# Attention units taken two by two, routing once per batch, and the experts' second layer with activations stationary

## The chip, the cores and the metric

The kernel runs on one core of a Trainium2 chip, in float32 throughout. The metric is the device time of one execution in microseconds. Five engines share the work, each with an instruction queue of its own that it follows in order: TensorE (PE in the profile; PEld is its loading of weights), VectorE (DVE), ScalarE (ACT), GpSimd (POOL) and SyncE (SP), which here only issues DMAs.

## The reference, cut to what matters

Banded attention with a few global keys is followed by a mixture of experts, in which each token goes to the one expert with the largest logit.

```python
# q, k, v: (4, 8, 768, 64); keep = key < 8, or 0 <= query - key < 96
scores = scale * q @ k.T - slope[h] * dist            # masked where not keep
x = softmax(scores) @ v                               # -> (3072, 512), heads side by side
logits = x @ w_gate                                   # 8 experts
e = argmax(logits);  gate_w = softmax(logits)[e]
y = relu(x @ w1[e]) @ w2[e]                           # 512 -> 1024 -> 512, for each token's expert
out = gate_w * y
```

## The kernel before, in words

**Attention.** The work is cut into 48 units: 4 batches times 4 pairs of heads times 3 groups of 256 queries. A queue of loads on SyncE (`load`, line 376, eight DMAs a pair for q and k; `load_v`, two) runs three pairs ahead in two buffers. VectorE turns a pair's q and k (`turn_qk`, lines 436 and 437), ScalarE makes copies of the keys and values (`keys_at`, `turn_v`). A unit passes through `scores` (line 484: matmuls of 64 rows, for two heads at once on the two halves of the array's rows; then the exponential on ScalarE, line 487, and the product with the decay on VectorE, lines 494 and 498), two units later through `attend` (line 516, then VectorE's normalization, lines 520 and 523), and two later through `turn` (line 532: two transposes on TensorE of the unit's rows; the copy, line 535, is ScalarE's). The last pair of heads of each group stores the rows to the DRAM table `x_tok` (`store`, line 236) and computes the logits (`logits`, line 547: w_gate as 32-column weights on the four column quarters of the array, one per chunk of 128 features; `logits_sum`, line 560, adds the four quarters with a matmul). Where a batch is complete, `gate` (lines 211 to 229) takes the argmax and the gate weight.

**Routing.** `spread` (line 567 on) makes each token's place in its expert's list: prefix sums over the batch by matmuls with a triangle (line 572), with ones for each earlier chunk of the batch (line 574) and for earlier batches (line 578), then some ten small VectorE steps and two larger one-hot tables (lines 603 and 608). `spread_sum` (line 624) sums the tables into `acc`. After the last batch, `order` ranks experts 1 to 7 by their number of tokens, so that the list of capacities `CAPS` (line 22: 464, 416, 416, 400, 400, 368, 368, 272) can be static; experts are run in the order of `ORDER` (line 23). `half_0`/`fetch_0` gather the rows of expert 0, in two lots; `take(1)` those of the next expert, once `settle` and `rows_of` have made its indices.

**The order of the instructions** is written out by hand in `banded_attention` (from line 733 on, the loop at line 744). Behind the last unit, 16 pieces of expert 0's first 256 slots (`work`, `hidden_0` line 320 and `result_0` line 327) are dealt out between the steps of the routing, so that TensorE has something to do while VectorE and the DMAs work.

**Experts.** The remaining 208 slots of expert 0 and the seven other experts follow (lines 999 to 1107). `hidden` (line 1039): 32 products, w1 stationary, all slots of the expert moving, Relu by ScalarE (line 1041). `result` (line 1082): w2 stationary, hidden activations moving, so that the output comes out with features on the partitions; VectorE copies it to `yT` (line 1084), and TensorE transposes it back by blocks of 128 slots (`turn`, line 1072), which happens during the next expert's `hidden`. `finish` scales by the gate weight (line 309) and scatters the rows to the output (`put`, line 301, an indirect DMA of GpSimd).

Rows of the expert after the next are gathered by GpSimd, 32 slots times four feature chunks per DMA (`gather_one`, line 259), each made to wait for a step of the present expert (`pace`); `sort` (line 270, VectorE transposes) turns them into the operand of `hidden` and stands between `hidden` and `result`. Weights lie in two buffers, `w_first` and `w_second`; SyncE loads the next expert's by an index that it reads from `ids_s` (`fetch`, lines 240 and 1024, five DMAs of 4 MB in all), w1 as soon as `hidden` has done with the buffer and w2 as soon as `result` has. For expert 1 the load waits for the index and for half of its gathers.

Of the kernel before, what the change touches and what calls it, by code (L numbers as in the profile page):

```python
# [16 lines left out]
P = 128  # L17
# [6 lines left out]
NQ = 4  # L24
# [5 lines left out]
def kernel(  # L30
# [27 lines left out]

    x_tok = nc.dram_tensor("x_tok", (N * NJ, P), F32)
# [22 lines left out]
    q_first = consts.tile([P, NB, 2, D], F32)  # L82
# [48 lines left out]

    tokid = consts.tile([P, NC], F32)
    iota(tokid, [[P, NC]], -N, 1)
# [5 lines left out]
    def later_constants():  # L139
# [13 lines left out]
        nc.vector.tensor_copy(out=j_of, in_=j_i)  # L153
        nc.vector.memset(wg_sb, 0.0)
        nc.sync.dma_start(wg_sb[:, :, 0:E], moe_w_gate.rearrange("(kc p) e -> p kc e", p=P))

    gsum = sel[:, 0:E]

    M_ec = consts.tile([P, E, NC], F32)
    M_ce = consts.tile([P, NC, E], F32)  # L160
    rk_all = consts.tile([P, NB, E + 1], F32)
    nc.vector.memset(rk_all[:, :, E:E + 1], 0.5)
    Macc = consts.tile([P, E], F32)
# [8 lines left out]
    NR = E - 1  # L172
# [5 lines left out]
    idx_0 = [consts.tile([P, 1, 2], I32, name=f"idx_0{i}") for i in range(2)]  # L178
    gslot_0 = [consts.tile([P, 1, 2], F32, name=f"gslot_0{i}") for i in range(2)]
    rows_0 = [consts.tile([P, 2 * TB], I32, name=f"rows_0{i}") for i in range(2)]  # L180
# [75 lines left out]

    def gather_one(xq, cols, i, top=N):
# [16 lines left out]
    def plan(p):  # L274
        if p < E:
            r = ORDER[p] - 1
            xqs[p] = xq_s[p % 2]
            cols = rows_s[:, NQ * TB * r:NQ * TB * r + NQ * TB]
            for i in range(pieces_of(CAPS[r + 1])):
                pending.append((xqs[p], cols, i))  # L280
# [10 lines left out]
    taken = []  # L291

    def take(p):
        plan(p)
        while pending:
            taken.append(gather_one(*pending.pop(0)))

    scatters = []

    def put(y, rows, where):  # L300
        p = nc.gpsimd.indirect_dma_start(out=out[:, :], out_offset=bass.IndirectOffsetOnAxis(ap=where, axis=0),  # L301
                                         in_=y[0:rows, :], in_offset=None, bounds_check=N - 1, oob_is_err=False)
# [4 lines left out]
    def scaled(name, rows, po, gs, where, later=None):  # L307
        y = yp.tile([P, DM], F32, tag="y", name=name)
        nc.vector.tensor_scalar(out=y[0:rows, :], in0=po[0:rows, :], scalar1=gs[0:rows, :], scalar2=None, op0=ALU.mult)  # L309
        if later is None:  # L310
            put(y, rows, where[0:rows, :])
        else:
            later.append(lambda: put(y, rows, where[0:rows, :]))

# [9 lines left out]
    def result_0(po, q, f0, nf, later=None):  # L324
# [4 lines left out]
        if f0 + nf == FC:  # L329
            scaled(f"y_0_{q}", P, po, gslot_0[0][:, 0, q:q + 1], idx_0[0][:, 0, q:q + 1], later)  # L330
# [18 lines left out]
    def banded_attention():  # L349
        with ExitStack() as actx:  # L350
            mp = actx.enter_context(tc.tile_pool(name="maskb", bufs=1))
            xlp = actx.enter_context(tc.tile_pool(name="xlb", bufs=3))
            xrp = actx.enter_context(tc.tile_pool(name="xrb", bufs=5))
            ldp = actx.enter_context(tc.tile_pool(name="ldb", bufs=2))
# [821 lines left out]
```

## Time and profile before

| | us |
|---|---|
| three timed runs | 543.27, 543.34, 544.06 |
| span of the profiled execution | 555.3 |
| first unit of attention to the last, by the chain | 5 to 178 |
| routing of the last batch beside expert 0's first 256 slots | 178 to 214 |
| expert 0's rest, and experts 1 to 7 | 214 to 548 |
| the end | 548 to 555 |
| VectorE, ScalarE and GpSimd busy, of the span | 201.7, 132.6 and 138.3 |

The page's fifth part lists groups of instructions by line and shape with their count, busy time, and the mean time of one. Matmuls overlap in the pipeline, so the mean time of one is longer than the distance between two starts; that distance is read from the chain or the timeline, as the length of a run divided by its count. Each float32 product is two matmul instructions in these lists, and each transpose on TensorE is one. The list of waits gives, for each pair of a waiting group and the group that released it, the total, the number of times and the longest. The stretches of the experts' stage in the chain alternate: `ph` (hidden), `pt` (the transposes back) and `po` (result).

### The profile page before, as it was taken

To read this page: it belongs to the slowest core of one execution; us is meant where nothing else is said; L and a number is where in the kernel's file an instruction comes from. 1 tells how busy PE (TensorE), PEld (TensorE's weight loads), DVE (VectorE), ACT (ScalarE), POOL (GpSimd) and SP (SyncE) were. 2 spreads that over 40 slices of the span, in tenths; PEclk is the share of its full clock that TensorE was granted. 3 is DMA by queue.
4 is the path that set the end of the run, shared out by engine and by line. 5 is a ranking of instruction groups with operands and counts; after the bars stand their busy time and mean duration, and the time that the engine had idled before them with its cause. 6 is when DMAs were issued, how large, how long until landed. Compare 5 with 4: busy or idle time off the path is not lost.

```text
span 555.3 us, 8124 instructions
## 1 busy us (share of the span) xinstructions
PE 527.4 (95%) x3130; PEld 391.7 (71%) x3130; DVE 201.7 (36%) x509; ACT 132.6 (24%) x263; POOL 138.3 (25%) x161
## 2 busy tenths in 40 slices
PE   4999999999999998599999999999999999999994
PEld 3988898899898965595555555555555876666694
DVE  4758687687684443112013101211301303111012
ACT  4666456555552200101101100100110100101100
POOL 5000000000007067234224423513511716402002
PEclk9999999999999999699999999999999999999998
DMA  9999999999903014995446174372543776101001
GB/s 145 146 156 178 234 176 175 231 161 159 256 6 124 31 30 93 297 187 201 98 90 223 34 159 141 114 156 70 183 107 64 234 147 216 48 0 53 3 1 60
DMA packets 145185, 71.97 MB, mean 130 GB/s; under 512 B 126656, under 2 KB 126660, under 8 KB 145136
## 3 DMA queue, kind: packets, MB, share of 16 engines
q1 hardware_dynamic: 137344, 58.16, 50.0%
q0 software_dynamic: 5264, 12.59, 7.5%
q10 hardware_dynamic: 2528, 0.59, 0.7%
q8 instruction: 27, 0.44, 0.4%
q14 instruction: 22, 0.18, 0.1%
HBM read 59.00 MB, written 12.65 MB: 129 GB/s over the span
## 4 chain that ended last, share of the span: by engine, by line
PE 85%; DMA 5%; SPq 2%; issue 2%; DVE 2%; another core or an unknown queue 2%; POOL 1%; ACT 0%; POOLq 0%; DVEq 0%; ACTq 0%
PE po L1082 26%; PE ph L1039 26%; PE o L516 12%; PE s L484 7%; PE ph L320 3%; PE px L532 3%; PE po L327 2%; PE pt L1072 2%; SPq L384 2%; DMA xq_s<-x_tok,rows_s 2%; DMA kb<-in_k_dram 1%; PE pq L547 1%; PE pi L624 1%; PE pl L560 1%
## 5 line engine op out<-in xcount | busy, mean ns | idle before, releaser
L259 POOL DMA_INDIRECT xq_s<-x_tok,rows_s x85 | 85.4, 1005 | 151.4 <-DVE yT L1084 103.6
L1041 ACT ACTIVATE hT<-ph 128x416 f32<-128x416 f32 (+4 forms) x64 | 29.6, 467 | 294.3 <-PE ph L1039 270.1
L1039 PE MATMUL ph<-xe,w_first 128*128 128x208 f32 (+3 forms) x256 | 78.7, 465 | 8.9 <-ACT hT L1041 8.9
L1082 PE MATMUL po<-hT,w_second 128*128 128x416 f32 (+4 forms) x320 | 80.7, 412 | 2.1 <-DVE yT L1084 2.1
L1039 PE MATMUL ph<-xe,w_second 128*128 128x416 f32 (+3 forms) x256 | 80.2, 469 | 0.0
L1082 PE MATMUL po<-hT,w_first 128*128 128x208 f32 (+3 forms) x256 | 75.5, 456 | 0.0
L1082 PEld LDWEIGHTS po<-hT,w_second 128*128 128x128 f32 x320 | 56.0, 190 | 26.3 <-issue 10.2
L1039 PEld LDWEIGHTS ph<-xe,w_first 128*128 128x128 f32 x256 | 49.0, 197 | 35.2 <-issue 10.0
L516 PE MATMUL o<-vt,e 128*128 128x128 f32 x384 | 72.6, 278 | 0.0
L1039 PEld LDWEIGHTS ph<-xe,w_second 128*128 128x128 f32 x256 | 48.0, 190 | 28.1 <-issue 9.9
L1082 PEld LDWEIGHTS po<-hT,w_first 128*128 128x128 f32 x256 | 47.7, 190 | 27.1 <-issue 10.2
L270 DVE STREAM_TRANSPOSE xe<-xq_s 128x128 f32<-128x128 f32 x85 | 22.8, 293 | 117.7 <-DMA xq_s<-x_tok,rows_s 112.5
L516 PE MATMUL o<-va,e 128*128 128x128 f32 x320 | 62.8, 278 | 0.0
L1084 DVE COPY yT<-po 128x416 f32<-128x416 f32 (+6 forms) x36 | 17.0, 481 | 125.6 <-PE po L1082 125.6
L259 POOL DMA_INDIRECT xq<-x_tok,rows x15 | 17.3, 1154 | 181.0 <-DVE early L648 160.5
L516 PEld LDWEIGHTS o<-vt,e 128*128 128x128 f32 x384 | 57.5, 194 | 1.5 <-issue 1.2
L487 ACT ACTIVATE e<-s 128x1024 f32<-128x1024 f32 (+1 forms) x48 | 45.5, 947 | 46.1 <-PE s L484 46.0
L516 PEld LDWEIGHTS o<-va,e 128*128 128x128 f32 x320 | 48.7, 193 | 2.6 <-issue 2.5
L301 POOL DMA_INDIRECT out_dram<-y,idx_s x25 | 24.4, 975 | 74.4 <-DVE y L309 69.9
L498 DVE TENSOR_TENSOR e<-e,Wb 128x1024 f32<-128x1024 f32 x32 | 38.8, 1211 | 10.9 <-ACT e L487 10.8
L484 PE MATMUL s<-qT,kT 64*128 64x128 f32 x384 | 40.7, 290 | 0.9 <-ACT qT L419 0.9
L484 PE MATMUL s<-qT,kA 64*128 64x128 f32 x320 | 35.7, 301 | 2.0 <-ACT kA L403 2.0
(163 smaller groups left out, 439.1 us busy)
## 6 DMA issues: line engine op xcount, KB each, us to landing
w_second<-in_moe_w_dram SPq DMA_DIRECT2D x16, 512.0 KB
w_second<-in_moe_w_dram SPq DMA_DIRECT2D x4, 2048.0 KB
x_tok<-xr SPq DMA_DIRECT2D x24, 256.0 KB
w_first<-in_moe_w_dram SPq DMA_DIRECT2D x12, 512.0 KB
w_first<-in_moe_w_dram SPq DMA_DIRECT2D x3, 2048.0 KB
vt<-in_v_dram SPq DMA_DIRECT2D x31, 192.0 KB
qb<-in_q_dram SPq DMA_DIRECT2D x60, 96.0 KB
kb<-in_k_dram SPq DMA_DIRECT2D x60, 96.0 KB
```

The costliest lines, as they stand in the source:

```text
L259: return nc.gpsimd.indirect_dma_start(out=xq[:, i, :], out_offset=None, in_=x_tok[0:NJ * top, :], in_offset=bass.IndirectOffsetOnAxis(ap=c ...
L270: nc.vector.transpose(xe[:, :, 32 * i:32 * i + 32], xq[:, i, :].rearrange("p (k q) -> p k q", k=KC))
L301: p = nc.gpsimd.indirect_dma_start(out=out[:, :], out_offset=bass.IndirectOffsetOnAxis(ap=where, axis=0), in_=y[0:rows, :], in_offset=None ...
L320: nc.tensor.matmul(ph[:, P * f:P * f + P], lhsT=w1_0[:, 0, kc, c0:c0 + P], rhs=xe_0[:, kc, P * q:P * q + P], start=(kc == 0), stop=(kc == ...
L484: nc.tensor.matmul(ps[:, h, P * m:P * m + P], lhsT=lhsT, rhs=qT[r, P * i:P * i + P], start=True, stop=True)
L487: nc.scalar.activation(e[:, :, 0:w], ps[:, :, 0:w], AF.Exp, scale=D ** -0.5)
L498: nc.vector.tensor_tensor(out=eh, in0=eh, in1=W[:, 2 * j:2 * j + 2, P:3 * P].rearrange("p h (o c) -> p h o c", o=1).to_broadcast([P, 2, 2, ...
L516: nc.tensor.matmul(po[:, t, h, :], lhsT=pt[:, h, P * m:P * m + P], rhs=(vt if own else va)[:, c0:c0 + P], start=(m == mine[0][0]), stop=(m ...
L1039: nc.tensor.matmul(ph[:, 0:C], lhsT=w1t[:, 0, kc, P * fc:P * fc + P], rhs=xe[:, kc, 0:C], start=(kc == 0), stop=(kc == KC - 1))
L1041: done = nc.scalar.activation(hT[:, fc, 0:C], ph[:, 0:C], AF.Relu)
L1082: nc.tensor.matmul(po[:, 0:c1 - c0], lhsT=w2t[:, 0, fc, P * dc:P * dc + P], rhs=hT[:, fc, c0:c1], start=(fc == 0), stop=(fc == FC - 1))
L1084: pace(2 if dc == 0 else 1, nc.vector.tensor_copy(out=yT[:, dc, c0:c1], in_=po[:, 0:c1 - c0]))
```

## The change

It touches three places.

1. *Attention.* Units go two at a time: scores of both, then one `turn` with four transposes for the pair before, then `attend` of the two units before. The logits are computed once per batch, with w_gate as 32-column weights over four quarters of the batch's tokens, accumulated over the four feature chunks; one VectorE transpose brings tokens to the partitions (so tokens are numbered differently, which `tokid` follows). A VectorE scan makes the counts of earlier chunks and batches, so that `spread` needs two products instead of six or seven. The tables of `spread` become a step of their own (`tables`). Expert 0's weights are loaded from unit 12 on, w1 first.

2. *Expert 1 takes a fixed place*, like expert 0: its weights are loaded by `expert_w1(w1_1, ...)` near the end of attention without an index, and its rows come with the second lot of expert 0's. The buffers of these weights exist from the start; before they are filled, attention keeps q and k, the first pair's q, a mask, the transposed rows and every fourth tile of exponentials in them.

3. *Second layer.* In `result`, blocks of 128 slots of the hidden activations are stationary and all 512 columns of w2 move, so the output has slots on the partitions and needs no transposing back. A remainder of up to 96 slots is done in pieces of 32 slots: four matmuls for four quarters of the features, each with 32-column weights and 128 moving columns, whose outputs lie in the four quarters of the partitions; such a piece is scattered by rows of 128 features. `sort` of the next expert moves from before `result` into it, in parts behind the second and third blocks; there are two buffers of hidden activations instead of one, and gathers are paced two to a block.

The diff, cut to its core:

```diff
+            def logits(b):
...
                 for kc in range(KC):
+                    for g in range(TB):
+                        nc.tensor.matmul(pq[32 * g:32 * g + 32, :], lhsT=wg_sb[:, kc, :], rhs=xl[:, kc, QS * g:QS * g + QS],
+                                         start=(kc == 0), stop=(kc == KC - 1))
+                L = gp.tile([P, QS], F32, tag="L", name=f"L_{b}")
+                nc.vector.transpose(L, pq)
...
             def spread(b):
...
                 nc.tensor.matmul(pr, lhsT=tri, rhs=Mb, start=True, stop=False)
-                for c in range(NB - 1):
-                    nc.tensor.matmul(pr[:, c + 1:NB, :], lhsT=ones,
...
+                nc.tensor.matmul(pr, lhsT=ones, rhs=C_b[b][:, :, 0:NB].rearrange("p e c -> p c e"), start=False, stop=True)
...
-            for n in range(nu + 1):
...
+            for n0 in range(0, nu, 2):
+                two = (n0, n0 + 1)
...
+                if n0 > 0 and c < 2 and pr + 1 < B * NJ:
+                    turn_qk(pr + 1)
+                for n in two:
...
                     scores(n)
...
+                if n0 >= 4:
+                    turn(n0 - 4)
+                    for n in two:
+                        attend(n - 2)
+                if b > 0 and m == 2:
+                    logits(b - 1)
+                if b > 0 and m == 4:
+                    spread(b - 1)
+                if 0 < b and m == (4 if b == B - 1 else 6):
+                    tables(b - 1)
+                if 0 < b and m == (6 if b == B - 1 else 8):
+                    spread_sum(b - 1)
...
+            turn(nu - 2)
+            expert_w1(w1_1, slice(1, 2))
+            work(1)
+            logits(B - 1)
+            nc.sync.dma_start(w2_1, w2v[:, 1:2, :, :])
+            work(1)
...
             def result(p):
...
+                rest = C % P if C % P <= 3 * 32 else 0
+                nq = (C - rest + P - 1) // P
+                for q in range(nq):
+                    rows = min(P, C - P * q)
+                    po = ps_o.tile([P, DM], F32, tag="po", name=f"po_{p}_{q}")
+                    for fc in range(FC):
+                        nc.tensor.matmul(po[0:rows, :], lhsT=hT[:, fc, P * q:P * q + rows], rhs=w2t[:, 0, fc, :],
+                                         start=(fc == 0), stop=(fc == FC - 1))
+                    pace(2, finish(p, q, rows, po))
+                    if p > 0 and q > 0:
+                        sort(p + 1, q - 1, nq - 1)
+                for i in range(TB * nq, pieces_of(C) if rest else 0):
+                    pt = ps_t.tile([P, P], F32, tag="pt", name=f"pt_{p}_{i}")
+                    for fc in range(FC):
+                        for g in range(TB):
+                            nc.tensor.matmul(pt[32 * g:32 * g + 32, :], lhsT=hT[:, fc, 32 * i:32 * i + 32],
+                                             rhs=w2t[:, 0, fc, P * g:P * g + P], start=(fc == 0), stop=(fc == FC - 1))
+                    finish_piece(p, i, pt)
...
             ground()
-            sort(1)
+            sort(1, 0, 1)
             hidden(0)
+            fetch(2, 0)
             plan(2)
-            turn = result(0)
+            result(0)
+            fetch(2, 1)
...
             for p in range(1, E):
-                hidden(p, turn)
-                fetch(p + 1, 0)
-                sort(p + 1)
+                hidden(p)
+                fetch(p + 2, 0)
                 plan(p + 2)
-                turn = result(p)
-                fetch(p + 1, 1)
+                result(p)
+                fetch(p + 2, 1)
```

`hidden` also zeroes the slots that fill up its last piece, and `gates_of`, in the routing's tail, adds two small matmuls that bring the gate weights into the pieces' order.

## The prediction

> **What bounds the kernel now.** I read the page's parts 1 and 4 first, then the table of groups by shape, then TensorE's timeline of the attention stage and VectorE's around the one long wait.
>
> ```profile
> PE 527.4 (95%) x3130; PEld 391.7 (71%) x3130; DVE 201.7 (36%) x509; ACT 132.6 (24%) x263; POOL 138.3 (25%) x161
> PE 85%; DMA 5%; SPq 2%; issue 2%; DVE 2%; another core or an unknown queue 2%; POOL 1%; ACT 0%; POOLq 0%; DVEq 0%; ACTq 0%
> ```
>
> TensorE is busy for 95% of the span and is 85% of the chain that ended last. Its idle gaps over 0.15 us sum to 15.2 us: 3 at the start, 8.9 at 220, 2.06 at 457, little else. So time comes out mainly where TensorE's own instructions go away, or run side by side. Busy time overlaps in a pipeline, so I price a matmul by its pace, the distance from one start to the next. In the chain, 64 matmuls of 416 columns take 22.35 us (349 ns each); 400 columns take 336 ns, 368 take 309, 208 take 176, 512 take 429. That is 0.84 ns a column, with a floor near 112 ns: 128-column matmuls and the 8-column ones of line 560 alike. (A float32 product is two such instructions, a transpose is one.)
>
> ```profile
> 50.43 0.44 PE L532 MATMUL px<-ident,xr 128*128 128x128 f32 x2
> 50.70 0.39 PE L516 MATMUL o<-va,e 128*128 128x128 f32 x2
> ...
> 52.27 0.39 PE L516 MATMUL o<-vt,e 128*128 128x128 f32 x2
> 52.58 0.49 PE L484 MATMUL s<-qT,kA 64*128 64x128 f32 x4
> 52.91 0.39 PE L484 MATMUL s<-qT,kT 64*128 64x128 f32 x4
> 53.13 0.39 PE L484 MATMUL s<-qT,kA 64*128 64x128 f32 x4
> 53.35 0.39 PE L484 MATMUL s<-qT,kT 64*128 64x128 f32 x4
> 53.67 0.44 PE L532 MATMUL px<-ident,xr 128*128 128x128 f32 x2
> 54.04 0.64 PE L547 MATMUL pq<-xl,wg_sb 128*32 128x256 f32 x8
> 54.61 0.71 PE L516 MATMUL o<-vt,e 128*128 128x128 f32 x4
> ```
>
> Two things are to be seen. Four scores start every 0.22 us, but 0.33 passes after the first four of a unit, and 0.31 between the last pair of o and the first scores: a change of the array's shape costs about 0.1 us at each edge. And eight logit matmuls of 256 columns fit into 0.57 us, though one alone paces at 216 ns: with 32-column weights on four quarters, four run at once.
>
> ```profile
> DVE xe L270 <- DMA xq_s<-x_tok,rows_s: 112.5, 44, 10.8
> ...
> ACT hT L1041 <- remote: 10.2, 1, 10.2
> ...
> PE ph L1039 <- ACT hT L1041: 8.9, 1, 8.9
> ```
>
> The lines are from the list of waits (total, times, longest). The last two are one event at 218 us: ScalarE stands still after the first Relu of expert 0's rest, for a reason the trace does not name, and TensorE with it; TensorE's clock then is 0.50 from 222.6 for 10.2 us. It costs 8.9 + 2.2 = 11.1 us. The profiled span is 555.3, the three timed runs are 543.3 to 544.1; 555.3 - 11.1 = 544.2. I read the event as not being in the timed runs, and carry my sum to 543.3. The first line's longest is the wait at 457: VectorE sat 10.8 us on a gather that landed late, beside a load of weights, with the copies of yT queued behind.
>
> [...]
>
> **The change, attention stage (38 to 214 us).**
> (a) Two units in one go: scores, scores, four transposes, attend, attend. Per pair one set of edges goes: 0.19 at the scores, 0.05 at px, 0.09 at the end of o, together 0.34 us (a full unit now is 1.09 + 0.27 + 1.88 = 3.24, without edges 2.9). 24 pairs, the first one or two not in this order: 22 x 0.34 = -7.5.
> (b) Logits once per batch. Now each of 12 pays 0.10 (px to pq) + 0.57 + 0.44 (pl) = 1.11, 13.3 in all. Then, four times, 8 rounds of four 192-column matmuls at 0.161 plus 0.25 of edges: 6.2. -7.1. The pl sums become one VectorE transpose per batch.
> (c) Prefix sums: 54 matmuls of lines 572 to 578 at 0.11 become 16. -4.2.
> (d) gates_of: two small matmuls, four instructions with edges, +0.6.
> (e) Tail: spread of the last batch now also waits for the scan, behind a transpose and eight gate steps of about 0.24: 2.8 us after the logits, with one piece of fill (16 x 0.112 = 1.8) before it: +1.0; two gaps of 0.3 go: -0.6.
> (f) What a faster TensorE runs into. VectorE has 31.6 us busy in the batch from 81 to 123 (42.0 us), and 69 instructions with about 0.04 between them: 34 us of the 37 that are left (42.0 less 2.0, 1.8 and 1.1 of a to c). Gate, spread and tables (about 5.5 us) come in three iterations of some 6 us, two of which also turn the next pair (1.9). The transposes of the next iteration leave some 1.2 us of slack, so I take +1 a batch, three times. In the first batch the loads of pair 3 set the pace until 38 us: +1 of (a) not won. SyncE issues loads for four pairs, weights and stores in 41 us (67.1 to 108.3) almost without a break; loads end 8.6 to 11.6 us ahead of use and took 3.5 to 4.8 to land, so two or three batches can eat the lead: +1. Sum +5; 0 if the queues have room, 11 if VectorE or SyncE becomes the bound.
> Weights of expert 0 come from unit 12 on. Those of expert 1, five DMAs and 4 MB, go on SyncE's queue without an index at about 165 (the stage's end, 178, less 13), behind the last stores: nothing on the path, since the loads at 217 were needed only at 237 (as hidden(0) and result(0) would run undisturbed). SBUF shared with w1_second and w2_second: the readers are done two iterations before the next writer, 0. Expert 0's last seven gathers now run partly beside those 4 MB: seven at 1.3 us and 2 to land are 11 us, TensorE has 17 of fill, 0; landing as late as the one at 457 it would be +4 (in the 11). Expert 1's thirteen stay behind them on POOL, 0.
> Sum: -7.5 - 7.1 - 4.2 + 0.6 + 0.4 + 5 = **-12.8**.
>
> **The change, expert stage.** A block of 128 slots is 16 matmuls of 512 columns, 6.87 us (line 327 does just this: 429 ns). A piece is 16 rounds of four 128-column matmuls: 16 x 0.112 + 0.3 of edges = 2.1; between 1.8 and, with every load of weights exposed (0.22 a round), 3.8. Transposes of yT, 108 at 0.109, are gone, and a part-filled piece is paid whole:
> - expert 0's rest (208): 11.25 + 0.87 becomes 6.87 + 5.7 (three pieces): +0.4
> - 416, twice: 22.35 + 1.74 becomes 20.6 + 2.1: -1.4 each
> - 400, twice: 21.49 + 1.74 becomes 22.7: -0.5 each
> - 272: 14.7 + 1.3 becomes 15.8: -0.1, and the wait of 2.06 goes, for the sort now comes 14 us later: -2.1
> - 368: 19.8 + 1.3 becomes 20.6: -0.5; the last one, 20.9 + 1.3 becomes 20.6: -1.6
> Sum -7.7 (-5.6 and -2.1). Against it: the second half of the next expert's sort now stands behind the last block's scaling, and hidden(p + 1) needs all of it. Scaling starts 0.2 after the block and takes 0.75; transposes follow at 0.197. With seven of them: 2.5 us after the block against a piece of 2.1, +0.4, three times; with five, 0; for 272 all twelve stand there: 3.5, +1.4; behind 368 no piece covers six: +2.3. Sum +4.9. VectorE loses the 36 copies (17 us); its pieces and memsets hide under matmuls. Gathers paced two to a block, and one more scatter for a piece, leave GpSimd 17 DMAs at 1.3 us in an expert's 44 us: hidden. Stage: **-2.8** (-8 to +5).
>
> Total -15.6: 543.3 - 15.6 = **527.7**; against the profile's own span, 544.2 - 15.6 = 528.6, or 539.7 if the event at 218 comes back.
>
> **The rivals.**
> A, the sum: 527.7, own range 521 to 535; chance 0.60.
> B, the queues bind. VectorE in order, or SyncE, takes 11 instead of 5, and pieces cost 3 instead of 2.1 (8 x 0.9): 527.7 + 6 + 7.2 = 541; half of that excess gives 534. For it: VectorE at 34 of 37 us. Against: its load is uneven but its waits are short. Chance 0.20.
> C, the event at 218 is in the timed runs too, tied to the load of w_second that starts then and now comes 40 us earlier: 527.7 - 11.1 = 516.6. For it: SyncE's steps are slow in just those 10 us. Against: 555.3 - 11.1 fits the timed runs. Chance 0.12.
> D, slower: the quarters do not overlap at 128 columns, so a piece is 64 x 0.112 = 7.2 us. Eight pieces: +41, 568. It decides from 2.1 + 15.6 / 8 = 4.05 us a piece. For it: nothing here shows 128-column rounds. Against: 256-column rounds pace at 0.22 for four, and 128-column scores, two at once on halves of the rows, at 0.112 for two. Chance 0.08.
>
> A measurement of this kernel can tell about 0.2% from no change, 1.1 us. Faster 0.89 (A, C, most of B), same 0.03 (the rest of B), slower 0.08. The range goes from C into B, 516 to 538, and leaves out D and the worse part of B.
>
> **What would show it.** Right: two units of scores in a row, a pair at about 6.1 us; attention's last matmul before hidden(0) about 13 us earlier; eight pieces near 2.1 us; waits of 0.4 to 2.3 us before hidden(2), hidden(6), hidden(7) on the transposes of xe; no pt on yT. Wrong: starts of a piece's matmuls 112 ns apart one by one; TensorE waiting in attention for e, xr or kT by more than 2 us a batch; hidden(1) waiting for w_second.

## The result, and the profile after

| | before | after |
|---|---|---|
| timed runs, median (range) | 543.70 us (543.27 to 544.06) | 535.64 us (535.03 to 536.54) |
| ratio, 95% interval | | 0.9854 (0.9836 to 0.9871) |
| span of the profiled execution | 555.3 | 533.1 |

The change wins 8.1 us, where 15.6 were forecast. The experiments were run in five further sittings, each beside the kernel before; it took 545.2, 545.8, 557.0, 558.4 and 558.4 us in them, so numbers are compared within one sitting only, or as ratios.

The page of the kernel after begins:

```profile
PE 503.7 (94%) x3244; PEld 344.4 (65%) x3244; DVE 179.6 (34%) x482; ACT 127.5 (24%) x227; POOL 140.1 (26%) x163
...
PE 85%; DVE 5%; DMA 3%; SPq 3%; ACT 2%; issue 1%; POOL 0%; POOLq 0%; ACTq 0%
```

TensorE still sets the time. It is busy 20.1 us less than in the undisturbed profile of the kernel before (523.8, the first experiment below), although 114 more matmuls run; in the pieces and in the logits four run side by side (they start 7 ns apart, and a round of four comes every 109 ns with 128 columns and every 163 with 192). TensorE's timeline of a stretch of attention (start, duration, instruction, count):

```profile
92.81 1.51 PE L573 MATMUL pq<-w_second,wg_sb 128*32 128x192 f32 x32
94.25 0.49 PE L507 MATMUL s<-qT,kA 64*128 64x128 f32 x4
...
95.91 0.39 PE L507 MATMUL s<-qT,kT 64*128 64x128 f32 x4
96.23 0.66 PE L559 MATMUL px<-ident,xr 128*128 128x128 f32 x4
96.73 0.39 PE L542 MATMUL o<-va,e 128*128 128x128 f32 x2
...
99.85 0.34 PE L589 MATMUL pr<-M_b,tri 128*128 128x48 f32 x2
100.02 0.40 PE L590 MATMUL pr<-C_b,ones 128*128 128x48 f32 x2
100.35 0.49 PE L507 MATMUL s<-qT,kT 64*128 64x128 f32 x4
```

The logits of a whole batch take 1.44 us to the next scores. The transposes come four at a time, once per pair, and two products make the prefix sums. The list of waits (total, times, longest) and the chain (start, duration, group) show the expert stage:

```profile
PE ph L1065 <- DVE xe L295: 4.3, 5, 2.0
...
DVE xe L295 <- DMA xq_s<-x_tok,rows: 3.4, 4, 1.0
...
PE pt L1103 <- issue: 2.7, 1, 2.7
```

```profile
211.02 6.87 PE po L1094 x16
217.88 4.38 PE pt L1103 x153
222.26 2.65 issue
224.91 2.25 PE pt L1103 x39
227.17 0.52 PE pf L1115 x2
227.69 22.91 PE ph L1065 x64
...
436.34 0.75 DVE y L335
437.23 1.08 DVE xe L295 x6
438.39 1.05 DVE xe L295 x5
439.48 20.05 PE ph L1065 x64
...
480.22 0.62 issue
480.84 1.28 DVE xe L295 x6
482.16 20.05 PE ph L1065 x64
```

Two things cost TensorE its time here. Before five of the hidden layers it waits for the sort, 4.3 us in all: at 436 the twelve transposes stand on the path behind the scaling of the block. That was in the forecast. And in expert 0's third piece it stops after 153 of 192 matmuls, for 2.65 us, and waits for nothing that the profile shows ("issue"). That was not. VectorE's old wait of 112.5 us on gathers is down to 3.4, for the sort now comes later in VectorE's queue, behind blocks of the second layer. The page also names two DMA queues of the kind `instruction`: q8 with 27 packets and 0.44 MB, 16 KB each, and q14 with 22 packets and 0.18 MB, 8 KB each. "Fetches of instructions" below are their packets.

### The profile page after: what moved, and what is told of

Its sections match the earlier page's. It is cut to its first block, busy times and chain, and to the rows that moved or that the text cites. A ratio compares the mean times of both kernels' runs of the same rounds, so it can differ in the third digit from the quotient of the medians.

```text
span 533.1 us, 8244 instructions
## 1 busy us (share of the span) xinstructions
PE 503.7 (94%) x3244; PEld 344.4 (65%) x3244; DVE 179.6 (34%) x482; ACT 127.5 (24%) x227; POOL 140.1 (26%) x163
## 4 chain that ended last, share of the span: by engine, by line
PE 85%; DVE 5%; DMA 3%; SPq 3%; ACT 2%; issue 1%; POOL 0%; POOLq 0%; ACTq 0%
PE ph L1065 29%; PE po L1094 27%; PE o L542 12%; PE s L507 6%; PE ph L347 2%; PE px L559 2%; PE po L354 2%; DMA vt<-in_v_dram 2%; SPq L409 2%; PE pt L1103 2%; DVE xe L295 1%; PE pq L573 1%; PE pi L632 1%; DVE e L524 1%; DMA k_first<-in_k_dram 1%
## 5 line engine op out<-in xcount | busy, mean ns | idle before, releaser
L284 POOL DMA_INDIRECT xq_s<-x_tok,rows_s x72 | 72.8, 1010 | 61.8 <-ACT hT L1067 49.6
L335 DVE TENSOR_SCALAR y<-po,gslot_s 128x512 f32<-128x512 f32 (+1 forms) x17 | 12.8, 751 | 223.7 <-PE po L1094 223.7
L1094 PE MATMUL po<-w_second,hT 128*128 128x512 f32 (+1 forms) x176 | 76.2, 592 | 0.0
L1094 PE MATMUL po<-w_first,hT 128*128 128x512 f32 (+1 forms) x160 | 69.3, 592 | 0.0
L1065 PEld LDWEIGHTS ph<-xe,w_first 128*128 128x128 f32 x256 | 47.5, 190 | 29.6 <-issue 10.3
L1094 PEld LDWEIGHTS po<-w_second,hT 128*128 128x128 f32 (+1 forms) x176 | 33.2, 189 | 41.3 <-issue 40.7
L542 PE MATMUL o<-vt,e 128*128 128x128 f32 x288 | 54.6, 281 | 0.0
L1094 PEld LDWEIGHTS po<-w_first,hT 128*128 128x128 f32 (+1 forms) x160 | 30.2, 189 | 37.4 <-issue 36.9
L542 PE MATMUL o<-va,e 128*128 128x128 f32 x240 | 47.2, 279 | 0.0
L542 PEld LDWEIGHTS o<-vt,e 128*128 128x128 f32 x288 | 43.9, 198 | 0.2 <-issue 0.2
L507 PEld LDWEIGHTS s<-qT,kT 64*128 64x128 f32 x384 | 29.7, 193 | 2.2 <-ACT qT L444 1.3
```

The costliest lines, as they stand in the source:

```text
L284: return nc.gpsimd.indirect_dma_start(out=xq[:, i, :], out_offset=None, in_=x_tok[0:NJ * top, :], in_offset=bass.IndirectOffsetOnAxis(ap=c ...
L335: done = nc.vector.tensor_scalar(out=y[0:rows, :], in0=po[0:rows, :], scalar1=gs[0:rows, :], scalar2=None, op0=ALU.mult)
L507: nc.tensor.matmul(ps[:, h, P * m:P * m + P], lhsT=lhsT, rhs=qT[r, P * i:P * i + P], start=True, stop=True)
L542: nc.tensor.matmul(po[:, t, h, :], lhsT=pt[:, h, P * m:P * m + P], rhs=(vt if own else va)[:, c0:c0 + P], start=(m == mine[0][0]), stop=(m ...
L1065: nc.tensor.matmul(ph[:, 0:C], lhsT=w1t[:, 0, kc, P * fc:P * fc + P], rhs=xe[:, kc, 0:C], start=(kc == 0), stop=(kc == KC - 1))
L1094: nc.tensor.matmul(po[0:rows, :], lhsT=hT[:, fc, P * q:P * q + rows], rhs=w2t[:, 0, fc, :], start=(fc == 0), stop=(fc == FC - 1))
```

## The experiments

**The kernel before, undisturbed.** No edit; what was open is what of its first profile belongs to the timed runs.

> The kernel before, profiled once more, nothing changed. Theory 1: the event at 218 us (8.9 us of TensorE idle, then half clock) belongs to that one profiled execution; it does not show again, and the span is 541 to 542, some 2 below the timed 543.3. Rival: the event belongs to profiling, and the span is again 550 or more. Also open: whether the wait of 2.06 us at 457 on a late gather shows again; my sum counted its removal as a gain. Theory 1a: it does not, so 2 us of the forecast gain were never there; theory 1b: it does.

Measured: 545.01 us (ratio 0.9998, 0.9989 to 1.0007), span 542.9. Neither the stop of ScalarE at 218 nor the wait of 2.06 at 457 is there; TensorE's gaps after its first matmul sum to 5.4 us. So the event of 11.1 us was rightly left out, but the 2.06 us were as much an accident of that one execution, and the forecast credited the change with removing them. This profile is the right base for the ledger below.

**The old second layer with the new attention.** `result`, the place of `sort` and the buffers of hidden activations as before.

```diff
-                        nc.tensor.matmul(po[0:rows, :], lhsT=hT[:, fc, P * q:P * q + rows], rhs=w2t[:, 0, fc, :],
+                            nc.tensor.matmul(po[:, 0:c1 - c0], lhsT=w2t[:, 0, fc, P * dc:P * dc + P], rhs=hT[:, fc, c0:c1],
```

> The changed kernel with the second layer and the sort of the kernel before (w2 stationary, yT copied and transposed back, whole sort between hidden and result, one buffer of hidden activations). Theory 1: attention and routing give some 14 us, the new second layer gives nothing or costs 1 to 3 us (the third piece of expert 0 waited 2.65 us, waits on sorts 4.35 us, filled-up pieces): 532 to 535, hidden(0) starting at about 200 as in the changed kernel. Rival: the second layer is worth the 2.8 us that I forecast and attention gives less: about 538 to 539.

Measured: 531.19, ratio 0.9733 (0.9709 to 0.9758). The stage from expert 0's rest to TensorE's last matmul takes 319.9 us, exactly as in the kernel before (319.9); with the new second layer it takes 323.2. The whole gain, and more, comes ahead of this stage. Expert 1's fixed place, which this run keeps, changes nothing in its length.

**Expert 0's rest in two blocks instead of a block and three pieces.**

```diff
-                rest = C % P if C % P <= 3 * 32 else 0
+                rest = C % P if C % P <= 3 * 32 and p > 0 else 0
```

> The changed kernel, but the remaining 208 slots of expert 0 are done as two blocks of 128 and 80 slots instead of one block and three pieces. Theory 1: [...] (2.65 us, then half clock for 3.4 us); two blocks take 13.75 us against the 16.2 measured, and hidden(1) runs at full clock: 2.5 to 4 us faster than the changed kernel, 532 to 533. Rival: the wait is for something else (a gather, a weight) that ends at the same time whatever runs: TensorE waits elsewhere, 535 to 536.

Measured: 530.72, ratio 0.9748 (0.9721 to 0.9775). Two blocks take 13.7 us where block and pieces took 16.2, the half clock of 3.4 us behind is gone (mean granted clock 0.995, against 0.983 in the changed kernel), the five waits stay. The stage takes 319.9, 3.3 less than in the changed kernel. By the ratios the run is some 6 us below the changed kernel, more than the 2.5 to 4 expected; the end is shorter too, 8.5 us instead of 10.3, which the last experiment takes up.

**The sort one block earlier**, so that a full block always follows the last part.

```diff
-                    if p > 0 and q > 0:
-                        sort(p + 1, q - 1, nq - 1)
+                    if p > 0 and q < nq - 1:
+                        sort(p + 1, q, nq - 1)
```

> The changed kernel with each part of the next expert's sort one block earlier (behind the first and second blocks instead of the second and third). Theory 1: the waits before hidden(2), (3), (4), (6) and (7), 0.34, 0.34, 0.34, 1.3 and 2.03 us, go, all sorts being done before the last block ends: 4 us faster than the changed kernel, 531 to 532. Rival: at the earlier place the gathers have not landed (they are issued up to the end of hidden and land up to 10 us later beside weights); VectorE waits with the scaling queued behind, and the gain is under 1 us or a loss.

Measured: 531.29, ratio 0.9735 (0.971 to 0.976). All five waits are gone, and the gathers are in time for it; the stop in the third piece is there, with 3.20 us. Its chain:

```profile
224.03 3.20 issue
...
406.90 1.89 PE pt L1103 x64
408.79 14.86 PE ph L1065 x64
423.65 13.73 PE po L1094 x32
437.38 1.89 PE pt L1103 x64
439.27 19.98 PE ph L1065 x64
```

Piece follows block and hidden layer follows piece without a break. A piece takes 1.89 us.

**The changed kernel again**, beside the next three.

> The changed kernel itself, as the base for the other runs. Theory 1 (the sum of its own waits: 3.2 us longer in the expert stage and a tail 2.6 us longer than that of the kernel before): 8 us less than before, ratio 0.985, and 5 to 6 us more than the runs with expert 0's rest in blocks, with the sort one block earlier or with the old second layer, which were 14 us below before. Rival: the first sitting was not typical, and the ratio is 0.978 to 0.981 (10 to 12 us less), so that those three are worth only 2 to 4 us each.

Measured: 538.55 (534.62 to 540.01), ratio 0.9855 (0.9825 to 0.9885), the same as at first. Its profiled execution is one of the long ones, span 538.1: the stop in the third piece is 3.4 us, the granted clock is 0.50 for 6.8 us behind it, and for 3.4 us more behind the wait of 2.03 ahead of the last hidden layer. In the first profile the wait of 2.0 us at the same place was followed by none (the last section gives the idle times), so this changes from execution to execution, which may be why this kernel's times spread more (5.4 us here) than those of the kernel before (2.6).

**The load of w1 for expert 2 behind expert 0's pieces.**

```diff
             hidden(0)
-            fetch(2, 0)
             plan(2)
             result(0)
+            fetch(2, 0, last[-1])
```

`last[-1]` is the scaling of the last piece; each of the four loads waits for it. They come 12.7 us later than in the changed kernel beside this run, counted from the start of expert 0's rest.

> The loads of w1 for expert 2 are issued after the scaling of expert 0's last piece instead of at the end of its hidden layer, some 17 us later; nothing else differs. Theory 1 ([...] the fetch of its instructions shares the DMA engines with the 2 MB of weights): the idle time of 2.65 us before line 1103 in expert 0's third piece and the half clock after it go, three pieces take 5.7 to 6.2 us instead of 9.3, 3 to 4 us less than the changed kernel. Rival (three pieces in a row, 192 matmuls and 192 weight loads in 6 us, [...]): the idle time stays between 2 and 3.5 us, and the time is within 1 us of the changed kernel. Either way hidden(2) is not held up: its weights are needed only 45 us later.

Measured: 533.8 (533.36 to 534.67), ratio 0.9782 (0.9761 to 0.9802), 4.75 less than the changed kernel beside it. Its timeline on TensorE:

```profile
219.58 5.45 PE L1106 MATMUL pt<-w_first,hT 128*32 128x128 f32 x192
224.96 0.38 PE L1119 MATMUL pf<-bad,ones 128*128 128x1 f32 x2
225.20 1.29 PE L1067 MATMUL ph<-xe,w_second 128*128 128x416 f32 x3
```

192 matmuls in one go, 5.4 us for three pieces, no stop and no half clock behind. What differs shows in the DMA queues (packets, MB, share of the engines) in the first 4.6 us of the pieces, of the changed kernel first and of this one second:

```profile
q1 hardware_dynamic: 224, 0.80, 88.3%
q0 software_dynamic: 45, 0.18, 13.4%
q14 instruction: 1, 0.01, 0.8%
```

```profile
q0 software_dynamic: 101, 0.32, 19.7%
q8 instruction: 1, 0.02, 1.3%
q14 instruction: 1, 0.01, 0.4%
```

q1 is the load of weights, which takes 88% of all DMA time in the changed kernel; q8 is of the kind `instruction`. With the load behind, the fetch starts 1.5 us after the first piece does. With the load running it isn't there in 4.6 us: it starts 4.7 us after the first piece, takes 1.1, and TensorE goes on 1.3 us later. In all four profiles with such a stop (2.65 to 3.40 us) TensorE goes on 1.3 to 1.4 us after this fetch has ended. So the load brings the stop: this run shows that, for this sitting. That the late fetch is the link between them is argued from these times; that TensorE had no instructions left was not shown. That q8 is TensorE's is an estimate from counts: from one of its packets to the next, the last ones left out, TensorE starts 205 to 315 matmuls and loads of weights in the kernel before. In the changed kernel it starts 152 to 355, but 544 ahead of the late packet at 222.53 and 61 behind it. Pieces of 32 slots are the densest instructions of the kernel, 384 in 5.4 us, against 32 in a block's 6.9.

**Blocks for expert 0, the earlier sort, and the row numbers of expert 0 later.** The last part answers to two gaps of TensorE near 147 and 149, of 1.29 and 1.60 us. In the changed kernel VectorE is the reason; its timeline:

```profile
147.93 0.16 DVE L647 COPY gslot<-acc 128x2 f32<-128x2 f32 x1
148.00 1.22 DVE L524 TENSOR_TENSOR e<-e,Wb 128x1024 f32<-128x1024 f32 x1
149.13 0.95 DVE L520 TENSOR_TENSOR e<-e,Wb 128x768 f32<-128x768 f32 x1
150.00 0.22 DVE L271 TENSOR_SCALAR rows<-pw,j_of 128x8 int32<-128x8 f32 x1
```

In the last batch `tables`, `spread_sum`, `half_0` and the last `turn_qk` lie close together; VectorE runs without a break, and the product `pw` (line 270) and the transposes behind it, which need their buffer, wait in TensorE's queue ahead of attention that is ready.

```diff
-                if n0 == nu - 4:
-                    fetch_0(0)
-                    count_0()
                 if n0 >= 4:
                     turn(n0 - 4)
                     for n in two:
                         attend(n - 2)
+                if n0 == nu - 4:
+                    fetch_0(0)
+                    count_0()
```

> Expert 0's rest in blocks, the sorts one block earlier, and in the last batch the gathers' row numbers of expert 0 (two small matmuls and VectorE's steps) behind the two units of attention instead of ahead of them. Theory (the losses are additive, since each is idle time of TensorE): against the changed kernel 3.3 for expert 0, 4.35 for the waits before the five hidden layers, 2.9 for the two gaps near 147 and 149 and 1.7 for the half clock behind them, up to 1.7 from the tail: 12 to 14 us less, no gap over 0.3 us between 40 and 520 us. Rival (they hide each other: what comes earlier waits elsewhere, for a gather or for w1): only 6 us less, as each alone gave, with new gaps before a hidden layer.

Measured: 526.59 (524.4 to 527.46), ratio 0.9643 (0.9619 to 0.9668), 12.0 less than the changed kernel. The size was right and a part of it wrong: the gaps near 147 are gone, but a new one of 2.37 us stands before the last prefix sums, and expert 0's rest starts at 200.6, no earlier than in the runs without the move (198.9 to 202.4). Counted from the first scores, and against the changed kernel beside it, attention's last product comes 4.6 us earlier, and with it the load of expert 1's weights. But the last gather of expert 0's first lot is issued 1.9 us later and lands, beside that load, 5.9 us later (160.5 instead of 154.7); VectorE's transposes of expert 0's rows, which need the gathers, stand ahead of the logits:

```profile
165.09 0.31 DVE L295 STREAM_TRANSPOSE xe<-xq 128x128 f32<-128x128 f32 x1 [0.55 <-DMA xq<-x_tok,rows]
169.81 0.31 DVE L295 STREAM_TRANSPOSE xe<-xq 128x128 f32<-128x128 f32 x1 [4.41 <-DMA xq<-x_tok,rows]
170.05 0.34 DVE L576 STREAM_TRANSPOSE L<-pq 128x192 f32<-128x192 f32 x1
```

So the gain is the expert stage's and the end's: the stage takes 315.0 us in this kernel, 4.9 less than in the kernel before, and the end 8.3, 2.0 less than in the changed kernel.

**Units one by one**, all else as changed: `attend` of a unit comes between the scores of the next two.

```diff
                 for n in two:
                     ...
                     scores(n)
                     ...
+                    if n0 >= 4:
+                        if n == n0:
+                            turn(n0 - 4)
+                        attend(n - 2)
```

> Scores and attend alternate unit by unit again; the four transposes of a pair stay together, the logits stay once per batch. Theory 1 (the edges between tilings are paid per unit: 0.19 at the scores and 0.09 at the end of o): 22 pairs at 0.28, 6 us more than the changed kernel, and a pair of units takes 6.1 + 0.28 us. Rival (the queues, VectorE first, set the pace of a batch, and the edges lie under them): less than 2.5 us more.

Measured: 548.88 (544.38 to 551.07), ratio 1.0066 (1.0045 to 1.0088): slower than the kernel before, 10.3 more than the changed one beside it. The last product of attention starts 168.1 us after the first scores, instead of 157.0. Its timeline shows the edges, 0.33 from the first four scores to the next four or from the first o to the next, against 0.22 inside:

```profile
111.35 0.49 PE L507 MATMUL s<-qT,kA 64*128 64x128 f32 x4
111.67 0.39 PE L507 MATMUL s<-qT,kT 64*128 64x128 f32 x4
...
112.44 0.49 PE L542 MATMUL o<-va,e 128*128 128x128 f32 x2
112.77 0.39 PE L542 MATMUL o<-vt,e 128*128 128x128 f32 x2
...
114.42 0.49 PE L507 MATMUL s<-qT,kA 64*128 64x128 f32 x4
...
117.44 0.49 PE L507 MATMUL s<-qT,kT 64*128 64x128 f32 x4
```

From the first line to the last, the scores of two full units, four transposes and 28 matmuls of o, it takes 6.09 us. The same work takes 5.70 in the changed kernel and 6.05 in the kernel before, as the first scores of such a pair and of the next show (changed kernel first):

```profile
113.12 0.49 PE L507 MATMUL s<-qT,kA 64*128 64x128 f32 x4
...
118.82 0.49 PE L507 MATMUL s<-qT,kT 64*128 64x128 f32 x4
```

```profile
83.55 0.49 PE L484 MATMUL s<-qT,kA 64*128 64x128 f32 x4
...
89.60 0.49 PE L484 MATMUL s<-qT,kT 64*128 64x128 f32 x4
```

At 22 pairs, 0.39 is 8.6 of the 10.3 us, and the queues do not hide it. The pairs are not alike: three in a row take 0.39, 0.30 and 0.78 more than in the changed kernel, which at 22 pairs makes 10.8, the whole difference. Why the last of the three loses twice as much as the others I did not follow.

**The corrections together, in two sittings.** The first: pieces with the load behind them and the earlier sort.

> Expert 0's three pieces stay, w1 of expert 2 is loaded behind them, and the sorts come one block earlier. Theory (the losses add up): against the run with the load alone, 533.8, the five waits of 4.35 in all go and with them the half clock that followed the longest, 1.7: 528. Rival (the earlier sort then waits for its gathers, which were issued behind the same loads): 531 or more, with new waits for xe.

The same with the row numbers later, and one piece of fill moved from behind the last `tables` to ahead of the last `spread`:

> The kernel with pieces, load behind and earlier sorts, and the row numbers of expert 0 behind the two units of attention, and two pieces of fill instead of one between the last logits and the prefix sums (one instead of two later). Theory (the gap of 2.37 us before the last prefix sums and the half clock behind it came from VectorE's steps that were moved; 1.8 us of fill covers most of it): 3 to 4.5 us less than the same kernel without this move, 523.5 to 525. Rival (the chain over VectorE to the row numbers sets the start of expert 0 whatever TensorE does meanwhile): within 1 us of it, with the gap at another place between 160 and 200 us.

Blocks and the earlier sort:

> Expert 0's rest in blocks and sorts one block earlier, attention as in the changed kernel. Theory (the move of the row numbers gave back in the gap before the last prefix sums what it won at 147): within 1 us of the run with all three, 526.6. Against the kernel with pieces and the load behind them, one block of 6.87 for three pieces of 5.38 costs 1.5, and the end of the kernel, 2 us longer with the pieces, gives it back: within 1 us of it. Rival (the move was worth its 2.9 and 1.7): 530 to 531.

Blocks, earlier sort, row numbers later, fill moved:

> The run with all three, and two pieces of fill instead of one between the last logits and the prefix sums (one instead of two later). Theory: the gap of 2.37 before line 589 falls to some 0.6 and the half clock of 3.4 us behind it, 1.7, goes: 523 to 523.5. Rival (the chain over VectorE sets the start of expert 0): within 1 us of 526.6, the gap reappearing before line 279 or the transposes of expert 0's rest.

Measured, beside 556.97 for the kernel before: 547.62, 540.70, 541.37 and 535.20 (ratios 0.9826, 0.9714, 0.9717, 0.9612). All miss the numbers expected, for something else came in: in every one of these profiles ScalarE or VectorE stands still near expert 0's hidden layer, as ScalarE did in the first profile of the kernel before, and in the first two the second piece has stops although no weights are loaded beside it. So the first, third and fourth were put into another sitting, with the changed kernel beside them:

> The changed kernel once more, as base for the next three on their chip. In the last sitting the kernel before itself took 557.0, 11.2 more than in the two sittings ahead of it, and every kernel's ScalarE stood still in expert 0's hidden layer. Theory (that stall belongs to the chip and not to a kernel): where the kernel before takes 545, the changed kernel takes 537 to 538.5 and shows no idle ScalarE there; where it takes 557, both show it. Rival (it is tied to the order of the work): it comes and goes between kernels of one sitting.

> Three pieces, the load behind them, the sorts one block earlier, as before. Theory (late instructions in the third piece come from the load alone, and the slow rounds in this kernel's last profile from its chip): where the kernel before takes 545, three pieces take 5.4 to 5.7 us and the whole 527 to 528.5, some 10 us below the changed kernel. Rival [...]: three pieces take over 8 us again, and the whole over 531.

> Expert 0's rest in blocks, the sorts one block earlier, attention unchanged. Theory: 4.35 of waits and 1.7 for half clocks below the blocks alone, 526 to 528 where the kernel before takes 545. Rival: the sorts' gain is given back, over 530.

> As the last, with the row numbers of expert 0 behind two units of attention and the fill moved. Theory: in the last batch the two gaps (2.9 us) and the half clock behind them go: 3 to 5 us below the kernel without it, 522 to 524 where the kernel before takes 545. In the last sitting the two differed by 6.2. Rival (the chain over VectorE sets the start of expert 0): within 1 us.

| | us | ratio (95%) |
|---|---|---|
| before | 558.37 | |
| changed kernel | 552.46 | 0.9895 (0.9861 to 0.9929) |
| pieces, load behind, earlier sort | 545.01 | 0.9771 (0.974 to 0.9802) |
| blocks, earlier sort | 541.69 | 0.9686 (0.9656 to 0.9717) |
| blocks, earlier sort, row numbers later, fill moved | 532.50 | 0.9544 (0.9509 to 0.9579) |

The kernel before and the changed one are 13 and 14 us longer than in the quieter sittings, and the changed one too has such a stop, on VectorE's timeline:

```profile
207.82 0.75 DVE L335 TENSOR_SCALAR y<-po,gslot 128x512 f32<-128x512 f32 x1 [8.04 <-PE po L354]
```

The products of this block go on without a break from 196.4, eight of them to the end of the block, some 3.5 us; the scaling comes after 11.4. In the quieter run with all three corrections the same step comes 3.7 us after the same start (190.2). VectorE's transposes for the hidden layer stand behind it, TensorE waits 3.1 us for them, and ScalarE's first Relu comes 5.8 us after the layer's start instead of 1.7.

It is not this step alone: from the first scores to expert 0's rest the changed kernel takes 200.8 us here and 191.7 in its quieter sitting. At 192.9 and 198.6, too, VectorE starts 2.0 us after the product it needs has ended, where in the quieter run it follows within 0.04.

So the stop goes with the sitting, not with a kernel. (The sittings were on different chips, so the two cannot be told apart; the kernel before was not profiled in these.) It left one thing open: in these two sittings three pieces took 10.6 and 9.55 us with the load behind them, with stops of 0.3 us in the second piece, although the fetch came early (1.0 and 1.2 us after the first piece). The changed kernel in the second of them, with the load beside its pieces (88% of the DMA time again), took 9.64. So there the place of the load made no difference: that it holds up the pieces is shown for the quieter sitting alone. Dense pieces have a second weakness that these runs do not explain. The version without them and with the later row numbers is the best of all in both sittings: 20.0 us below the changed kernel here. How much the last step is worth in a quieter sitting wasn't measured; here it was 9.2 and before 6.2.

**Eight idle memsets on GpSimd.** The changed kernel ends 10.3 us after TensorE's last matmul, the kernel before 7.6. In the records of GpSimd's last semaphore instructions one stands 2.05 us behind the one ahead of it (4.44 and 6.49 us after TensorE's end), and a fetch of instructions, a packet of 8 KB on q14, starts at 4.77.

```diff
+    idle = consts.tile([P, 1], F32)
+    for _ in range(8):
+        nc.gpsimd.memset(idle, 0.0)
```

> The changed kernel with eight memsets of one column on GpSimd near the start, which nobody reads: they only push the rest of GpSimd's instructions back by eight. Theory (the 2.05 us by which GpSimd stands still between two of its last semaphore instructions, in the changed kernel and in no kernel with expert 0's rest in blocks, is a fetch of its next instructions that falls just there): with the code eight instructions further on [...] from TensorE's last matmul to the end of the span it takes 8.0 to 8.6 us instead of 10.2. Rival (the last semaphore waits for something that the three pieces cause, their scatters or the longer program of TensorE): 10.0 to 10.4 again. The third piece and the waits on the sorts are as in the changed kernel.

Measured: 550.15 beside 558.39 (ratio 0.985, 0.9817 to 0.9883). The end is 8.2 us, the two records stand 0.04 us apart. Moving GpSimd's code by eight instructions takes 2 us off the end, with all eight pieces in place; it isn't their scatters that cost it. The stop ends 1.3 us after the fetch has (5.19), as TensorE's stops did, which speaks for the fetch as its cause; whose instructions q14 carries, the views do not say.

## Why the forecast had the right sign and half the size

From the profiled execution of the kernel before in the second sitting (span 542.9) to that of the changed one (533.1):

| | forecast | profiles |
|---|---|---|
| up to the first scores | 0 | 9.1 to 7.0: -2.2 |
| first scores to expert 0's rest | -12.8 | 206.2 to 192.7: -13.6 |
| expert stage | -2.8 | 319.9 to 323.2: +3.3 |
| the end | 0 | 7.6 to 10.3: +2.7 |

The first row changes from execution to execution (the first scores came between 6.8 and 9.3 us); without it the sum is -7.6, against -8.1 timed. The 8.0 that are missing from the forecast are 4.1 for expert 0's rest, 2.7 for the end and 2.1 for a wait, less some 0.9 elsewhere.

**Attention held.** (a) A pair saves 0.35 (6.05 to 5.70) where 0.34 was taken, and taking the pairs apart cost 11.1 us at attention's end. (b) Logits: all their matmuls with edges take 5.75 us, forecast 6.2. (c) Sixteen matmuls of prefix sums take 2.3, forecast 1.8. (f) The charge of 5 for VectorE and SyncE was right in size and wrong in place: nothing a batch, but two gaps of 2.9 us together in the last one, and a half clock of 3.4 us behind them, 1.7 by estimate. There `tables` and `spread_sum` come two units earlier than in the other batches, and `half_0` with them.

**The expert stage did not**, and here the forecast lost 6.1 us:
- *The wait of 2.06 at 457, taken as removed: -2.1.* It was in one execution only. I tested the event of 11.1 us against the timed runs, and not this one; and that test compared a span with times. The disturbed execution was timed at 556.98 for its span of 555.3, 1.7 more. So 544.2 of span is 545.9 timed, some 2 us above the timed runs: this wait.
- *Expert 0's rest, +0.4.* That is the step that failed. It came to +4.0, and +0.5 in the half clock over the next hidden layer. The price of a piece was right: where nothing stops them, three take 5.4 us (5.7 forecast). The upper bound of 3.8 for one had a load of 32-column weights, 107 ns in the kernel before (190 for 128 columns), exposed in every round; a round takes 109 ns with its four loads. But the term put at nothing that TensorE could stop among them without waiting for data, as it did for 2.65 us. With the load of w1 for the expert after next moved behind the pieces the stop was gone, in that sitting; in the two slower ones the pieces had other stops, whose cause stays open.
- The rest nearly cancels: pieces at 1.9 instead of 2.1 (-1.0), waits of 4.35 instead of 4.9, of which each single one is within 0.3 of the forecast, and about +1.4 that is left, for the small product `pf` behind expert 0 (0.52 instead of 0.12) and edges of some 0.1 us between hidden layers, blocks and pieces.

**The end, taken as unchanged without a reason, is +2.7.** Moving GpSimd's code took 2.1 of it away; that the place of one fetch of instructions is the cause is argued, as above.

**The rivals.** B, that the queues bind, did not happen: pieces are cheaper than forecast and the batches run free but for the last. That the time came near the 534 which B names for half its excess is a coincidence. C, the stop at 218, fits no time of the quieter sittings; in the others such a stop is in the changed kernel's profile, and both kernels take longer there, so it is no property of either. D is out: four quarters start 7 ns apart and the next four 110 ns later. A is right in its mechanisms but for the terms above. The run with all three corrections, at 0.9643 where the forecast said 0.971, is no test of the sum: it does expert 0's rest in blocks, and it takes away the five waits, which the forecast had charged with 4.9.

## What to carry to other kernels

Blocks of activations as the stationary side saved 4.9 us of 320 here once nothing stood in the way, but only after the next expert's sort was given a whole block of matmuls to hide under and expert 0's rest was done in blocks: ask of every step that is moved what follows it, not only what went ahead. A stretch of many small matmuls is also a stretch of many instructions, 384 in 5.4 us here, and the DMA view counts their fetches (q8) and the load of weights (q1) on the same 16 engines. Keep large loads away from it (worth 4.75 us in the quieter sitting; in the slower one that had both, three pieces took 9.55 us without the load and 9.64 with it), or use the larger shape even if it computes some slots for nothing; of the two, the larger shape was the faster in both sittings that had them side by side. And a wait that is seen in one execution is a credit only after a second one shows it, or after the sum of the span is held against the timed runs with what the timing adds.

## What the runs showed of the hardware

- TensorE stopped for 2.65 to 3.4 us in the third of three pieces, waiting for nothing the profile shows, with 88% of the DMA time taken by a load and a fetch of instructions 3.2 us later than without it; there was no stop with the load 12.7 us later, in the sitting where it was measured.
- In the two profiles of the result the granted clock changes only at whole multiples of 3.413 us from its first rise: at 10.04, 13.45, 16.87, 149.99, 153.40, 225.08, 228.49 and 525.45 us in the changed kernel (13.45 and 149.99 lie 40 of them apart), at 17.79, 222.59, 232.83 and 550.27 in the kernel before. By the matmul records, TensorE was idle for 2.01, 2.61, 2.65 and 2.64 us of the step ahead of each half clock in the changed kernel, and for 2.55 and 2.73 in the kernel before, whose half clock of 10.24 us has 3.41 and 2.93 idle in its first two steps. No half clock follows the other steps between first rise and last matmul, whose idle time is 1.30 us at most. What happens between 1.30 and 2.01 these two do not show. So the wait of 2.03 us was followed by a half clock where it lay in one step (the changed kernel again, 2.03 idle), and by none where a border cut it (the first profile, 0.94 and 1.08). The gaps of 1.29 and 1.60 us gave one in the first profile (2.61 in one step), and none in the run with two blocks for expert 0's rest (1.35 and 1.55). The borders lie differently from execution to execution, the first rise 12.9 us after the first matmul in the kernel before and 5.1 in the changed one, which is luck for or against a kernel. In the third piece a matmul starts every 29 ns at full clock (153 in 4.38 us) and every 58 behind the stop (39 in 2.25, nearly all at 0.50). At half clock for 3.413 us, a gap of 2 us can cost 3.7, by estimate (2, and half of 3.413).
- Eight more instructions ahead of GpSimd's code went with an end of 8.2 us, where the first profile of the changed kernel has 10.3.
- In all nine profiles of three sittings ScalarE's first Relu of expert 0's rest came 5.0 to 11.9 us after the layer's start, instead of 1.7, for a reason that the traces do not name. The kernel before took 11 to 13 us more there, and the changed one, in the one of them that had it, 14. What causes it stays open.
